# Attention scores through two three-bank PSUM tiles, with one exp per three key tiles into a ring

## Chip, core and metric

The kernel runs on one core of one Trainium2 chip. The metric is the device time of one execution in microseconds (us), median of several runs; lower is better. A profiled execution gives a trace with the start and length of each instruction on the engines: TensorE (PE, with its weight loads as PEld), VectorE (DVE), ScalarE (ACT), GpSimd (POOL) and SyncE (SP).

## The reference

Attention with normalised queries and keys, followed by a mixture of experts in which each token goes to one expert by a hash of its id. Batch 8, 12 heads, 448 tokens, head size 64; 3584 tokens of width 768, 8 experts of width 1024.

```python
q_n, k_n = (rmsnorm(q, g_q), rmsnorm(k, g_k))
scale = 1.0 / np.sqrt(q.shape[-1])
scores = scale * np.matmul(q_n, k_n.transpose(0, 1, 3, 2))
scores = scores - np.max(scores, axis=-1, keepdims=True)
attn = np.exp(scores)
attn = attn / (np.sum(attn, axis=-1, keepdims=True) + 1e-09)
return np.matmul(attn, v).astype(np.float32)
...
expert_idx = token_ids * np.int64(2654435761) % np.int64(E)
out = np.zeros((N, D), dtype=np.float32)
for e in range(E):
    mask = expert_idx == e
    if not mask.any():
        continue
    xe = x[mask]
    h = np.maximum(xe @ w1[e], 0.0)
    out[mask] = h @ w2[e]
```

## The kernel before

**Two stages.** First attention for all heads, with the routing tables computed beside it; then the experts, each with two matrix products over up to 512 gathered tokens. The attention result goes through a scratch tensor in HBM (`x_scratch`), is gathered per expert, turned by PE transposes, and the products are scattered to the output. The change lies in the attention stage.

**Steps and groups.** A step is one pair of heads of one batch element: 48 steps, `s` = 0 to 47. Steps come in groups, mostly of three, that share the preparation: squares of q and k on DVE (`prep_sq`), their sums by 16 matmuls against an identity on PE (`prep_sum`, line 287), a reduction on DVE (`prep_red`), an Ln and two exps on ScalarE (`prep_rr`), four products on DVE (`prep_norm`), and a copy of v (`prep_v`). For a group starting at step 3n the loop places one set of sums in the first and one in the second step of the group before or the one before that; a steady group of three steps therefore has two sets of sums, one Ln, and none in its third step.

**Scores.** The 448 keys of two heads make 3.5 tiles of 128 each. The kernel keeps them as seven key tiles per step (`SL = 7`): `score(s, j)` for j = 0, 1, 2 computes two tiles, one for each head, by two matmuls on 64 rows each, on the lower and on the upper half of the array (line 496); j = 3 computes the two half tiles as one matmul on all 128 rows (line 501). The scores go to a PSUM tile `sc_ps` of two banks, of which there are three. One exp takes both tiles of j = 0, 1, 2 (896 elements per partition, line 498), another the single tile of j = 3 (448, line 503). They write `expT`, one of two SBUF tiles of seven key tiles.

**AV.** `av_part(s, 0)` and `av_part(s, 1)` are 12 matmuls each (line 520), for one head each, `av_part(s, 2)` 8 more on half the columns (line 527), into the one PSUM tile `av_ps`; then DVE takes the reciprocal of the row sums and the product into `x_sb` (lines 535, 536). AV of a step runs one step after its scores.

**Transposes.** `transposes(s)` is eight PE transposes into the one PSUM bank `qkT_ps`, which it shares with the sums, and two DVE copies out of it, to kT and qT (lines 485, 487).

**Order.** It is written by hand (`manual_schedule`); each engine takes its instructions in that order in this loop. In step s (lines 688 to 709): scores j = 1 and 2, transposes of s + 1, score j = 3, AV parts 0 and 1 of s - 1, the `pre` and `mid` lists (v, squares, norms, sums), AV part 2 of s - 1, score j = 0 of s + 1, the `post` list (Ln and exps of `prep_rr`). So the six matmuls of j = 0, 1, 2 stand together on PE. After that, from step 14 on, one entry of `side` per step: eleven parts p1 to p11 of the routing, fourteen pairs of table columns (`table`, one DVE and one POOL operation for each column), and `table_mm` (28 matmuls). p3, p6 and `table_mm` each use a `sc_ps` tile. POOL issues the loads of q, k, v and weights and the gathers.

**PSUM.** Eight banks: six for `sc_ps`, one for `qkT_ps`, one for `av_ps`.

Of the kernel before, what the change touches and what calls it, by code (L numbers as in the profile page):

```python
# [8 lines left out]
FP32 = mybir.dt.float32  # L9
BF16 = mybir.dt.bfloat16  # L10
FP16 = mybir.dt.float16
I32 = mybir.dt.int32
AF = mybir.ActivationFunctionType
ALU = mybir.AluOpType
AX = mybir.AxisListType
PSUM = bass.MemoryType.PSUM
# [3 lines left out]
def kernel(  # L20
# [12 lines left out]
    nc = tc.nc  # L33

    B, H, S, D = q.shape
    N, DIN = out.shape
    E = moe_w1.shape[0]
    F = moe_w1.shape[2]
    P = 128
    HP = H // 2  # L40
    CO = DIN // P
    FO = F // P
    NTC = N // P
    HW = DIN // 2
    scale = 1.0 / float(D) ** 0.5
# [6 lines left out]
    NHI = E * KT + NOV  # L52
# [12 lines left out]
    SL = 7  # L65
# [129 lines left out]
            steps.append((gi, i))  # L195
    NG = len(groups)
    GMAX = 3

    with tc.manual_schedule(), \
         tc.tile_pool(name="a_nat", bufs=1) as a_nat, \  # L200
# [2 lines left out]
         tc.tile_pool(name="a_n8", bufs=2) as a_n8, \  # L203
         tc.tile_pool(name="a_v8", bufs=1) as a_v8, \
         tc.tile_pool(name="a_qk", bufs=3) as a_qk, \
         tc.tile_pool(name="a_exp", bufs=2) as a_exp, \
         tc.tile_pool(name="a_x", bufs=2) as a_x, \
         tc.tile_pool(name="rt_sb", bufs=1) as rt_sb, \
         tc.tile_pool(name="ps_qk", bufs=1, space=PSUM) as ps_qk, \
         tc.tile_pool(name="ps_sc", bufs=3, space=PSUM) as ps_sc, \  # L210
         tc.tile_pool(name="ps_av", bufs=1, space=PSUM) as ps_av:


# [3 lines left out]
        v_bufs = [a_nat.tile([P, 2 * HP, 8, D], BF16, name=f"vr_{t}") for t in range(NB)]  # L217
        v8_tiles = [a_v8.tile([P, GMAX, 8, DP], BF16, name=f"v8_{t}") for t in range(NV8)]

        first = a_exp.tile([P, SL, S], BF16, name="expT")[:].rearrange("p a s -> p (a s)")[  # L220
            :, 0:4 * 8 * D].bitcast(FP32).rearrange("p (a n s d) -> p a n s d", a=2, n=1, d=D)

        def runs(t, h0, hstep, nh, tok0, stride, cnt):
# [53 lines left out]
        def prep_sum(gi, a, wide=False):  # L277
            n = groups[gi][2]
            sq = st[gi].pop(("sq", a))
            m = 8 * n  # L280
            if wide:
                T = ps_sc.tile([P, 2, 512], FP32, name="sc_ps")[:, 0]
            else:
                T = ps_qk.tile([P, 512], FP32, name="qkT_ps")
            sp = T[:, 0:m * W].rearrange("p (s w) -> p s w", w=W)
            for c in range(NW):
                nc.tensor.matmul(sp, lhsT=ident16[:], rhs=sq[:, c, 0:m],  # L287
                                 start=(c == 0), stop=(c == NW - 1))
            st[gi]["sp", a] = sp
# [61 lines left out]
        slot_i = rt([P, NTC], I32, "slot_i")  # L351
        parts = rt([P, 2, NTC], I32, "parts")
        hl = rt([P, 2, NTC], FP32, "hl")
        lo1 = rt([P, NTC, P], FP16, "lo1")
        hi1 = rt([P, NTC, NHI], FP16, "hi1")
        V, G = nc.vector, nc.gpsimd
        rts = {}

# [13 lines left out]
            G.tensor_copy(oc[:], ot[:])  # L372

        def p3():
            ps = ps_sc.tile([P, 2, 512], FP32, name="sc_ps")[:, 0]
            oh = onehot[:].rearrange("p e c -> p (e c)")
            for h in range(2):
                nc.tensor.matmul(ps[0:KM, 2 * h:2 * h + 2], lhsT=oh[:, KM * h:KM * h + KM],
                                 rhs=sel2[:], start=True, stop=True)
            nc.tensor.matmul(ps[:, 8:8 + E], lhsT=emask[:], rhs=oc[:], start=True, stop=True)  # L380
            nc.tensor.matmul(ps[:, 8 + E:8 + 2 * E], lhsT=ones128[:], rhs=oc[:], start=True, stop=True)
            c4 = ps[0:KM, 0:4].rearrange("p (h k) -> p h k", k=2)
            V.tensor_copy(cmix[0:KM, :, 0:PL], c4[:, :, 0:1].to_broadcast([KM, 2, PL]))
            V.tensor_copy(cmix[0:KM, :, PL:P], c4[:, :, 1:2].to_broadcast([KM, 2, P - PL]))
            V.tensor_copy(et[:].rearrange("p a e -> p (a e)"), ps[:, 8:8 + 2 * E])  # L385
# [20 lines left out]
            G.tensor_tensor(out=add_e[:], in0=add_e[:], in1=base_e[:], op=ALU.subtract)  # L406

        def p6():
            ps = ps_sc.tile([P, 2, 512], FP32, name="sc_ps")[:, 0]
            oh = onehot[:].rearrange("p e c -> p (e c)")  # L410
            nc.tensor.matmul(ps[:, 0:E * NTC], lhsT=u128[:], rhs=oh, start=True, stop=False)
            for h in range(2):
                nc.tensor.matmul(ps[:, KM * h:KM * h + KM], lhsT=cmix[0:KM, h],
                                 rhs=tri[0:KM].rearrange("p e c -> p (e c)"),
                                 start=False, stop=(h == 1))
            V.tensor_tensor(out=rank[:], in0=ps[:, 0:E * NTC].rearrange("p (e c) -> p e c", e=E),
                            in1=bc(offl[:]), op=ALU.add)
# [27 lines left out]
                            scalar2=tv[:, c:c + 1], op0=ALU.is_equal, op1=ALU.mult)  # L445

        def table_mm():
            val = ps_sc.tile([P, 2, 512], FP32, name="sc_ps")[:, 0, 0:NHI]
            for c in range(NTC):
                nc.tensor.matmul(val, lhsT=lo1[:, c], rhs=hi1[:, c],  # L450
                                 start=(c == 0), stop=(c == NTC - 1))
            emp = rt([P, NHI], FP32, "emp")
            pos = rt([P, NHI], FP32, "pos")
            V.tensor_scalar(out=emp[:], in0=val, scalar1=0.0, scalar2=float(BIG),
                            op0=ALU.is_equal, op1=ALU.mult)
            V.tensor_scalar(out=pos[:], in0=val, scalar1=0.0, scalar2=-1.0,
                            op0=ALU.is_gt, op1=ALU.mult)
            V.tensor_tensor(out=emp[:], in0=emp[:], in1=pos[:], op=ALU.add)
            V.scalar_tensor_tensor(out=gidx[:], in0=val, scalar=float(N // 2), in1=emp[:],
                                   op0=ALU.add, op1=ALU.add)  # L460
# [20 lines left out]
        def transposed(s):  # L481
# [5 lines left out]
            nc.vector.tensor_copy(qT[:], T[:, 0:S])  # L487
            qkt[s] = (qT, kT)

        def score(s, j):  # L490
            qT, kT = qkt[s]
            expT = pend[s][0]
            sc = ps_sc.tile([P, 2, 512], FP32, name="sc_ps")
            if j < 3:
                for hh in range(2):
                    nc.tensor.matmul(sc[:, hh, :S], lhsT=kT[64 * hh:64 * hh + 64, P * j:P * j + P],  # L496
                                     rhs=qT[64 * hh:64 * hh + 64, :], start=True, stop=True)
                nc.scalar.activation(expT[:, 2 * j:2 * j + 2, :], sc[:, :, :S], AF.Exp,  # L498
                                     bias=0.0, scale=1.0)
            else:  # L500
                nc.tensor.matmul(sc[:, 0, :S], lhsT=kT[:, 384:512], rhs=qT[:, :],  # L501
                                 start=True, stop=True)
                nc.scalar.activation(expT[:, 6, :], sc[:, 0, :S], AF.Exp, bias=0.0, scale=1.0)  # L503
                qkt.pop(s)

        def av_part(s, part):
# [4 lines left out]
            if part == 0:  # L511
                av = ps_av.tile([P, SL, D + 1], FP32, name="av_ps")
                pend[s].append(av)
            expT, av = pend[s]
            tl = lambda hh, j: 6 if j == 3 else 2 * j + hh
            if part < 2:
                hh = part
                for t in range(3):
# [113 lines left out]
        side += [(lambda c=c: (table(c), table(c + 1))) for c in range(0, NTC, 2)]  # L632
        side += [table_mm]
        NS = len(steps)
        pend[0] = [a_exp.tile([P, SL, S], BF16, name="expT")]
        prep_sum(1, 0, True)
        prep_red(1, 0)
        score(0, 0)
# [10 lines left out]
        prep_v(0)  # L649
        transposed(1)  # L650
        zero_kv(nc.vector, v_bufs[0], HP, 2 * HP)
        pend[1] = [a_exp.tile([P, SL, S], BF16, name="expT")]
        score(1, 0)


# [27 lines left out]
        for s in range(1, NS):  # L683
            gi, i = steps[s]
            b, hp0, n = groups[gi]
            hp = hp0 + i
            nxt = s + 1 < NS
            score(s, 1)
            score(s, 2)
            if nxt:  # L690
                transposes(s + 1)
            score(s, 3)
            if s == NS - 1:
                for kt in range(KT - 1):
                    bank = ps_qk.tile([P, 512], FP32, name="qkT_ps")
                    put_xT(xg_e[kt], xT_e, kt, bank[:].bitcast(FP16)[:, 0:DIN])
            av_part(s - 1, 0)
            av_part(s - 1, 1)
            for f, *arg in pre[s]:
                f(*arg)  # L700
            for g, a in mid[s]:
                prep_sum(g, a)
                prep_red(g, a)
            av_part(s - 1, 2)
            if nxt:
                pend[s + 1] = [a_exp.tile([P, SL, S], BF16, name="expT")]
                score(s + 1, 0)
            for f, *arg in post[s]:
                f(*arg)
            if hp == 1 and b % 2 and b + 3 < B:  # L710
                load_qk(b + 3, 0, 2 * HP)
                load_v(b + 3, 0, 2 * HP)
            if side and s >= 14:
                side.pop(0)()
            if s == 24:
                n_ov = nc.values_load(novi[0:1, 0:1], min_val=0, max_val=NOV)
            if s == NS - 4:
                for kt in range(KT - 1):
                    gather(xg_e[kt], gidx[:, kt:kt + 1], N_EARLY)
            if hp == 3:  # L720
                if b == 3:
                    w_tiles[0] = [load_w1(0, w_pool)]
                if b == 4:
                    w_tiles[0].append(load_w2(0, w_pool))
                if b == 5:
                    w_tiles[1] = [load_w1(1, w_pool)]
                if b == 6:
                    w_tiles[1].append(load_w2(1, w_pool))
# [183 lines left out]
```

## Time and profile before

| | us |
|---|---|
| median of three runs (383.76 to 384.19) | 384.19 |
| the profiled execution | 386.59 |
| its span, first to last instruction | 385.0 |
| busy: PE, DVE, ACT, POOL | 344.5, 216.0, 187.5, 175.1 |
| attention steps with scores, first and last exp start | 12.8 to 185.53 |
| first to last Ln group read below, 12 groups of three steps | 49.04 to 171.21 |
| granted TensorE clock, 30 to 40 and 40 to 50 us | 0.74, 0.92 |

The profile page divides the span into 40 slices and prints tenths of busy time for each:

```profile
PE   7755998989999999999899999999998989999960
PEld 3443776766766777776667666666665656666630
DVE  5674789989999999988633233333222322232210
ACT  3753899989899999989321112212021111212200
```

A slice is 9.6 us. Up to about the nineteenth slice the core is in the attention stage, where PE, DVE and ScalarE are all near full; after it PE alone is. A matmul is recorded from its start to a modelled end, and matmuls overlap in the array, so distances between starts tell more about PE than busy time. The same holds in part for ScalarE and DVE, whose records overlap the next one's by some tenths of a microsecond.

### The profile page before, as it was taken

The page shows a single profiled execution, that of the slowest core. Times are in us where ns is not written, and L with a number is a line of the kernel's source. Part 1 is how long each engine was busy: PE and PEld are TensorE (multiplying, and loading weights), DVE is VectorE, ACT ScalarE, POOL GpSimd, SP SyncE. Part 2 cuts the span into 40 slices and gives each one's busy share as a digit, 9 for nine tenths or more (in the row PEclk, how much of TensorE's full clock was granted, in tenths as well). Part 3 has the DMA queues.
Part 4 walks back from the last instruction along what each step waited for, and adds up shares of the span by engine and source line. Part 5 has one row for each costly group of instructions (what it writes and reads, how often), then busy time and mean ns, then how long its engine had stood idle before and what let it go on. Part 6 is the DMA issues. An engine that isn't in the chain of part 4 may idle for free. (4 is left out here: it accounts for less than half of the span.)

```text
span 385.0 us, 9539 instructions
## 1 busy us (share of the span) xinstructions
PE 344.5 (89%) x4006; PEld 236.8 (62%) x4006; DVE 216.0 (56%) x519; ACT 187.5 (49%) x299; POOL 175.1 (45%) x247
## 2 busy tenths in 40 slices
PE   7755998989999999999899999999998989999960
PEld 3443776766766777776667666666665656666630
DVE  5674789989999999988633233333222322232210
ACT  3753899989899999989321112212021111212200
POOL 8998552014629950003347344462644636522030
PEclk9998899999999999999999999999999999999995
DMA  8999999943999999103548999999999999932030
GB/s 123 159 131 181 189 220 193 219 61 76 191 185 234 218 242 198 44 15 105 122 116 159 212 260 247 205 257 174 236 233 194 239 186 235 269 138 95 2 147 2
DMA packets 54269, 64.61 MB, mean 168 GB/s; under 512 B 22403, under 2 KB 42134, under 8 KB 53968
## 3 DMA queue, kind: packets, MB, share of 16 engines
q0 software_dynamic: 50592, 57.98, 85.8%
q1 hardware_dynamic: 3024, 5.41, 5.2%
q8 instruction: 32, 0.52, 0.6%
q10 hardware_dynamic: 608, 0.59, 0.5%
q14 instruction: 13, 0.11, 0.1%
HBM read 89.68 MB, written 18.09 MB: 280 GB/s over the span
## 5 line engine op out<-in xcount | busy, mean ns | idle before, releaser
L498 ACT ACTIVATE expT<-sc_ps 128x896 bf16<-128x896 f32 x144 | 123.9, 934 | 22.7 <-PE sc_ps L496 22.5
L765 PE MATMUL o_ps<-w_sb,h_sb 128*128 128x256 f16 (+1 forms) x512 | 87.9, 326 | 0.0
L752 PEld LDWEIGHTS <-w_sb 128*128 128x128 f16 x432 | 58.0, 144 | 25.7 <-issue 1.6
L752 PE MATMUL h_ps<-xT,w_sb 128*128 128x512 f16 x336 | 73.7, 379 | 0.0
L765 PEld LDWEIGHTS <-h_sb 128*128 128x128 f16 x512 | 48.9, 98 | 32.6
L173 POOL DMA_INDIRECT xg<-x_scratch,gidx x32 | 32.6, 1020 | 63.5 <-DVE x_sb L536 38.3
L770 POOL DMA_INDIRECT out_dram<-o_sb,gidx x32 | 33.0, 1031 | 51.5 <-ACT o_sb L769 17.0
L756 ACT ACTIVATE h_sb<-h_ps 128x512 f16<-128x512 f32 (+2 forms) x36 | 19.7, 550 | 75.1 <-PE h_ps L752 75.1
L758 DVE TENSOR_SCALAR h_sb<-h_ps 128x512 f16<-128x512 f32 (+2 forms) x36 | 22.8, 632 | 55.6 <-PE h_ps L752 55.6
L769 ACT COPY o_sb<-o_ps 128x768 f32<-128x768 f32 x16 | 12.8, 799 | 76.0 <-PE o_ps L765 51.3
L520 PEld LDWEIGHTS <-expT 128*128 128x128 bf16 x1152 | 42.5, 98 | 9.9 <-issue 6.0
L496 PE MATMUL sc_ps<-qT,kT 64*128 64x448 f16 x288 | 43.3, 358 | 4.5 <-DVE et L385 1.4
L520 PE MATMUL av_ps<-v,expT 128*128 128x65 bf16 x1152 | 44.0, 194 | 0.0
L769 DVE COPY o_sb<-o_ps 128x768 f32<-128x768 f32 x16 | 15.3, 958 | 45.7 <-PE o_ps L765 21.2
L816 POOL DMA_DIRECT2D w_sb<-in_moe_w_dram x36 | 23.1, 645 | 30.2 <-DMA w_sb<-in_moe_w_dram 28.2
L475 PE MATMUL qkT_ps<-ident,n 128*128 128x128 f16 x384 | 30.6, 222 | 5.4 <-DVE n L320 3.8
L475 PEld LDWEIGHTS <-n 128*128 128x128 f16 x384 | 22.3, 98 | 19.8 <-issue 11.9
L536 DVE TENSOR_TENSOR x_sb<-av_ps,srec 128x448 f16<-128x448 f32 x48 | 29.7, 619 | 1.5
L287 PEld LDWEIGHTS <-ident 128*128 128x128 f16 x544 | 24.6, 99 | 8.8 <-issue 6.8
L185 DVE COPY xT<-xT_ps 128x768 f16<-128x768 f16 x28 | 15.5, 554 | 23.9 <-PE xT_ps L184 23.8
L485 DVE TENSOR_SCALAR kT<-qkT_ps,g_col 128x512 f16<-128x512 f16 x48 | 23.1, 481 | 9.5 <-PE qkT_ps L475 8.4
L503 ACT ACTIVATE expT<-sc_ps 128x448 bf16<-128x448 f32 x48 | 27.7, 577 | 1.2 <-PE sc_ps L501 1.2
(140 smaller groups left out, 382.5 us busy)
## 6 DMA issues: line engine op xcount, KB each, us to landing
w_sb<-in_moe_w_dram POOLq DMA_DIRECT2D x32, 384.0 KB, 13.6
w_sb<-in_moe_w_dram POOLq DMA_DIRECT2D x12, 768.0 KB, 13.5
x_scratch<-x_sb SPq DMA_DIRECT2D x15, 288.0 KB, 6.1
w_sb<-in_moe_w_dram POOLq DMA_DIRECT2D x2, 1536.0 KB, 16.4
kr<-in_k_dram POOLq DMA_DIRECT2D x6, 384.0 KB, 9.0
qr<-in_q_dram POOLq DMA_DIRECT2D x3, 768.0 KB, 14.5
vr<-in_v_dram POOLq DMA_DIRECT2D x6, 384.0 KB, 19.4
kr<-in_k_dram POOLq DMA_DIRECT2D x6, 288.0 KB, 8.9
```

Source lines behind the costliest of these rows:

```text
L173: nc.gpsimd.indirect_dma_start(out=xg[:], out_offset=None, in_=x_dram[0:rows, :], in_offset=bass.IndirectOffsetOnAxis(ap=idx, axis=0), bou ...
L287: nc.tensor.matmul(sp, lhsT=ident16[:], rhs=sq[:, c, 0:m], start=(c == 0), stop=(c == NW - 1))
L475: nc.tensor.transpose(T[:, o:o + P], n8[:, a, i, j].rearrange("p h d -> p (h d)"), ident16[:])
L496: nc.tensor.matmul(sc[:, hh, :S], lhsT=kT[64 * hh:64 * hh + 64, P * j:P * j + P], rhs=qT[64 * hh:64 * hh + 64, :], start=True, stop=True)
L498: nc.scalar.activation(expT[:, 2 * j:2 * j + 2, :], sc[:, :, :S], AF.Exp, bias=0.0, scale=1.0)
L503: nc.scalar.activation(expT[:, 6, :], sc[:, 0, :S], AF.Exp, bias=0.0, scale=1.0)
L520: nc.tensor.matmul(av[:, 2 * t + hh, :], lhsT=expT[:, tl(hh, j), P * t:P * t + P], rhs=v8[:, i, 4 * hh + j, 0:D + 1], start=(j == 0), stop ...
L536: nc.vector.tensor_tensor(out=x_sb[:, :, hp * D:hp * D + D], in0=av[:, :, :D], in1=srec[:, :, None].to_broadcast([P, SL, D]), op=ALU.mult)
L752: nc.tensor.matmul(h_ps[:, :c1 - c0], lhsT=w1v[:, co, fo, :], rhs=xT[:, co, c0:c1], start=(co == 0), stop=(co == CO - 1))
L765: nc.tensor.matmul(o_ps[:, d0:d1], lhsT=h_sb[:, fo, col * P:(col + 1) * P], rhs=w2_sb[:, fo, d0:d1], start=(fo == 0), stop=(fo == FO - 1))
L769: (nc.vector.tensor_copy if col % 2 else nc.scalar.copy)(o_sb[:], o_ps[:])
L770: scat = nc.gpsimd.indirect_dma_start(out=out[:, :], out_offset=bass.IndirectOffsetOnAxis(ap=idx, axis=0), in_=o_sb[:], in_offset=None, bo ...
```

## The change

- The score tiles of all steps are numbered through, t = 7s + 2j + hh. Three successive ones share a PSUM tile of three banks (`GT = 3`), of which there are two. A tile that is begun in one step is finished in the next one where 7 is not a multiple of 3 (`filling` holds it).
- When the third is written, one exp takes all three (1344 elements per partition). Three steps then have seven exps instead of twelve, 112 in all instead of 192.
- The exps write one ring of 21 key tiles (`RING`), three steps' worth, in place of two tiles of seven. AV reads from the ring. The first group's raw q and k, which lay in an `expT` tile, lie in the ring.
- The order in a step: the transposes of s + 1 come between scores j = 1 and j = 2, score j = 3 between AV parts 0 and 1, and score j = 0 of s + 1 ahead of `pre`, `mid` and AV part 2. In the last step the three transposes of gathered tokens come ahead of score j = 3.
- The routing tables `lo1` and `hi1` lie in a weight tile of the pool that expert 0's and 1's second weights use.
- Users of a `sc_ps` tile other than scores (wide sums at the start, p3, p6, `table_mm`) take one of the two three-bank tiles.

```diff
@@ -195,6 +195,8 @@
     GMAX = 3
+    GT = 3
+    RING = GT * SL
@@ -203,11 +205,11 @@
-         tc.tile_pool(name="a_exp", bufs=2) as a_exp, \
+         tc.tile_pool(name="a_exp", bufs=1) as a_exp, \
...
-         tc.tile_pool(name="ps_sc", bufs=3, space=PSUM) as ps_sc, \
+         tc.tile_pool(name="ps_sc", bufs=2, space=PSUM) as ps_sc, \
@@ -217,7 +219,8 @@
-        first = a_exp.tile([P, SL, S], BF16, name="expT")[:].rearrange("p a s -> p (a s)")[
+        ring = a_exp.tile([P, RING, S], BF16, name="expT")
+        first = ring[:].rearrange("p a s -> p (a s)")[
@@ -279,7 +282,7 @@
-                T = ps_sc.tile([P, 2, 512], FP32, name="sc_ps")[:, 0]
+                T = ps_sc.tile([P, GT, 512], FP32, name="sc_ps")[:, 0]
@@ -351,8 +354,9 @@
-        lo1 = rt([P, NTC, P], FP16, "lo1")
-        hi1 = rt([P, NTC, NHI], FP16, "hi1")
+        tab = w_pool.tile([P, FO, DIN], FP16, name="w2_sb")[:].rearrange("p a b -> p (a b)")
+        lo1 = tab[:, 0:NTC * P].rearrange("p (c s) -> p c s", s=P)
+        hi1 = tab[:, NTC * P:NTC * (P + NHI)].rearrange("p (c s) -> p c s", s=NHI)
@@ -372,7 +376,7 @@
         def p3():
-            ps = ps_sc.tile([P, 2, 512], FP32, name="sc_ps")[:, 0]
+            ps = ps_sc.tile([P, GT, 512], FP32, name="sc_ps")[:, 0]
...
@@ -487,20 +491,22 @@
+        filling = []
+
         def score(s, j):
             qT, kT = qkt[s]
-            expT = pend[s][0]
-            sc = ps_sc.tile([P, 2, 512], FP32, name="sc_ps")
-            if j < 3:
-                for hh in range(2):
-                    nc.tensor.matmul(sc[:, hh, :S], lhsT=kT[64 * hh:64 * hh + 64, P * j:P * j + P],
-                                     rhs=qT[64 * hh:64 * hh + 64, :], start=True, stop=True)
-                nc.scalar.activation(expT[:, 2 * j:2 * j + 2, :], sc[:, :, :S], AF.Exp,
-                                     bias=0.0, scale=1.0)
-            else:
-                nc.tensor.matmul(sc[:, 0, :S], lhsT=kT[:, 384:512], rhs=qT[:, :],
-                                 start=True, stop=True)
-                nc.scalar.activation(expT[:, 6, :], sc[:, 0, :S], AF.Exp, bias=0.0, scale=1.0)
+            for hh in range(2 if j < 3 else 1):
+                t = SL * s + 2 * j + hh
+                if t % GT == 0:
+                    filling.append(ps_sc.tile([P, GT, 512], FP32, name="sc_ps"))
+                rows = slice(64 * hh, 64 * hh + 64) if j < 3 else slice(0, P)
+                nc.tensor.matmul(filling[0][:, t % GT, :S], lhsT=kT[rows, P * j:P * j + P],
+                                 rhs=qT[rows, :], start=True, stop=True)
+                if t % GT == GT - 1:
+                    r = (t + 1 - GT) % RING
+                    nc.scalar.activation(ring[:, r:r + GT, :], filling.pop()[:, :, :S], AF.Exp,
+                                         bias=0.0, scale=1.0)
+            if j == 3:
                 qkt.pop(s)
@@ -511,8 +517,9 @@
-            expT, av = pend[s]
-            tl = lambda hh, j: 6 if j == 3 else 2 * j + hh
+            av, = pend[s]
+            expT = ring
+            tl = lambda hh, j: (SL * s + (6 if j == 3 else 2 * j + hh)) % RING
@@ -686,25 +693,25 @@
             score(s, 1)
-            score(s, 2)
             if nxt:
                 transposes(s + 1)
-            score(s, 3)
+            score(s, 2)
             if s == NS - 1:
                 for kt in range(KT - 1):
                     bank = ps_qk.tile([P, 512], FP32, name="qkT_ps")
                     put_xT(xg_e[kt], xT_e, kt, bank[:].bitcast(FP16)[:, 0:DIN])
             av_part(s - 1, 0)
+            score(s, 3)
             av_part(s - 1, 1)
+            if nxt:
+                pend[s + 1] = []
+                score(s + 1, 0)
             for f, *arg in pre[s]:
                 f(*arg)
             for g, a in mid[s]:
                 prep_sum(g, a)
                 prep_red(g, a)
             av_part(s - 1, 2)
-            if nxt:
-                pend[s + 1] = [a_exp.tile([P, SL, S], BF16, name="expT")]
-                score(s + 1, 0)
             for f, *arg in post[s]:
                 f(*arg)
```

More of the change, by code (lines that the diff above doesn't have):

```diff
@@ L408, in p6 @@
         def p6():
-            ps = ps_sc.tile([P, 2, 512], FP32, name="sc_ps")[:, 0]
+            ps = ps_sc.tile([P, GT, 512], FP32, name="sc_ps")[:, 0]
             oh = onehot[:].rearrange("p e c -> p (e c)")
@@ L447, in table_mm @@
         def table_mm():
-            val = ps_sc.tile([P, 2, 512], FP32, name="sc_ps")[:, 0, 0:NHI]
+            val = ps_sc.tile([P, GT, 512], FP32, name="sc_ps")[:, 0, 0:NHI]
             for c in range(NTC):
@@ L634 @@
         NS = len(steps)
-        pend[0] = [a_exp.tile([P, SL, S], BF16, name="expT")]
+        pend[0] = []
         prep_sum(1, 0, True)
@@ L651 @@
         zero_kv(nc.vector, v_bufs[0], HP, 2 * HP)
-        pend[1] = [a_exp.tile([P, SL, S], BF16, name="expT")]
+        pend[1] = []
         score(1, 0)
```

## The prediction

> **What bounds the kernel now.** I read the windows first, cut at the exp that precedes each Ln on ScalarE (one Ln per head-pair group, three steps), to see which engine is full in the attention stage. The columns are start:end, length, then busy us and instruction count of PE, PEld, DVE, ACT and POOL, then granted clock, DMA share and GB/s.
>
> ```profile
> 69.17:78.97 9.80, 9.52 (x177) 6.92 (x173) 9.08 (x23) 9.28 (x16) 0.26 (x2) 1.00 1.54 219
> ...
> 141.04:150.83 9.79, 9.51 (x177) 6.92 (x173) 9.69 (x28) 9.27 (x15) 0.00 (x0) 1.00 1.09 222
> ...
> sum 122.17, PE 115.40 PEld 84.64 DVE 114.80 ACT 112.41 POOL 46.63; mean PE 9.62 PEld 7.05 DVE 9.57 ACT 9.37 POOL 3.89
> ```
>
> The second window shows DVE at its fullest. The sum line covers the twelve groups from 49.04 to 171.21 us. Three engines are nearly full, so a busy share decides nothing, and I went to the groups and then to the order in time.
>
> ```profile
> L498 ACT ACTIVATE expT<-sc_ps 128x896 bf16<-128x896 f32 x144 | 123.9, 934 | 22.7 <-PE sc_ps L496 22.5
> ```
>
> The 144 wide exps wait 22.5 us in all for score matmuls, over half of it before 43 us, while loads set the pace. In a steady group the wait is 0.49 us, once:
>
> ```profile
> 69.17 0.92 ACT L498 ACTIVATE expT<-sc_ps 128x896 bf16<-128x896 f32 x1 [0.45 <-PE sc_ps L496]
> ...
> 70.62 1.71 ACT L498 ACTIVATE expT<-sc_ps 128x896 bf16<-128x896 f32 x2
> 72.22 0.55 ACT L503 ACTIVATE expT<-sc_ps 128x448 bf16<-128x448 f32 x1
> 72.64 2.54 ACT L498 ACTIVATE expT<-sc_ps 128x896 bf16<-128x896 f32 x3
> 75.04 0.58 ACT L503 ACTIVATE expT<-sc_ps 128x448 bf16<-128x448 f32 x1
> ...
> 78.97 0.92 ACT L498 ACTIVATE expT<-sc_ps 128x896 bf16<-128x896 f32 x1 [0.49 <-PE sc_ps L496]
> ```
>
> ```profile
> 74.90 1.14 PE L496 MATMUL sc_ps<-qT,kT 64*128 64x448 f16 x6
> 75.97 0.62 PE L475 MATMUL qkT_ps<-ident,n 128*128 128x128 f16 x8
> 76.48 0.35 PE L501 MATMUL sc_ps<-qT,kT 128*128 128x448 f16 x1
> 76.67 0.91 PE L520 MATMUL av_ps<-v,expT 128*128 128x65 bf16 x24
> 77.47 0.85 PE L287 MATMUL qkT_ps<-sq_q,ident 128*128 128x96 f16 x16
> 78.25 0.32 PE L527 MATMUL av_ps<-v,expT 128*64 128x65 bf16 x8
> 78.50 0.74 PE L496 MATMUL sc_ps<-qT,kT 64*128 64x448 f16 x6
> ```
>
> Read together these show the ring that sets 9.80 us a group: ScalarE runs without a gap from 69.17 to the j=3 exp at 75.04; only its end frees the PSUM tile for the third pair of the burst at 74.90 (75.68 in the trace); PE then needs 2.82 us (transposes, j=3 score, 24 AV, 16 sums, 8 AV) to the next burst at 78.50, and the exp starts 0.47 later. 6.51 + 2.82 + 0.47 = 9.80. It is a ring through ScalarE, a PSUM tile and PE's order, not one engine. In steps without sums the period is 2.82 us (j=0 exps at 177.50, 180.32, 183.13), ScalarE alone.
>
> **What the Trainium skill says.** "ScalarE: Activation LUTs", section "What ACT_TABLE_LOAD costs": an ACTIVATE with immediates takes 186 ns + 0.833 ns per element, and neighbours overlap by about 93 ns. The trace agrees on the length (934 against 932) but shows more overlap: starts 0.797 us apart at 896 elements, 0.425 at 448, so a launch costs hardly anything beyond its elements. "TensorEngine Tiling (Array Packing)", section "Tiling Modes", Key Properties: changing the tiling mode drains TensorE. The trace agrees. The routing table's matmuls stand between two score pairs there:
>
> ```profile
> 160.16 0.36 PE L496 MATMUL sc_ps<-qT,kT 64*128 64x448 f16 x2
> 160.46 0.99 PE L450 MATMUL sc_ps<-hi,lo 128*128 128x64 f16 x28
> 161.38 0.36 PE L496 MATMUL sc_ps<-qT,kT 64*128 64x448 f16 x2
> ```
>
> Pair to full-array matmul takes 0.30 us where pair to pair takes 0.19, and the last of the 28 to the next pair takes 0.126 where their own spacing is 0.029: 0.10 us for each change of mode. "Perfetto Trace Analysis", section "Optimizing Scalar/DVE Operations": where ScalarE isn't saturated but causes bubbles elsewhere, smaller instructions let work finish sooner. The change goes the other way.
>
> **The change part by part.** *Fewer exps.* Three steps had nine exps of 896 and three of 448: 9 x 0.797 + 3 x 0.425 = 8.45 us; now seven of 1344, each 0.797 + 0.372 = 1.17: 8.19. With the 0.64 of Ln and rr the ScalarE floor goes from 9.09 to 8.83. At most 0.26 a group, if ScalarE were the bound.
>
> *PE's order.* The three score pairs of a step stood in one burst (0.68 us to the transposes); now s1 (first pair of the step), transposes, s2, half the AV, s3, other half, next step's s0, sums, last AV. Each lone pair changes mode on both sides. In starts: pair to what follows 0.29, transposes 0.45 + 0.10, AV half 12 x 0.031 = 0.37 (+ 0.10 ahead of a pair), s3 0.19, last AV 0.25, sums 0.78. A step is 0.29 + 0.55 + 0.29 + 0.37 + 0.19 + 0.47 + 0.29 + 0.25 = 2.70, a group with its two sums 9.66. Before: 0.68 + 0.51 + 0.19 + 0.80 + 0.78 + 0.25 = 3.21 twice and 2.47 without sums, 8.89. So PE's own work rises by 0.77 a group. The full-to-pair change after transposes and AV is not in the trace of before; its bounds are 0 and 0.10, and I take 0.10 from the routing table.
>
> *Two PSUM tiles in place of three.* The first matmul of a fill waits for the exp two fills back. From the last matmul of a fill to that release: 0.47 to the exp's start (78.50 to 78.97), 1.29 for the exp (0.92 + 0.37), 0.05 to PE (exp of 0.91 from 173.46, pair at 174.42): 1.81 us. Number a cycle's 21 tiles; fills are 0-2, 3-5, ... 18-20. PE's own way from a fill's last matmul to the first of the fill after next is: tile 20 to tile 3: s3 0.19, AV 0.47, s0 0.29, AV 0.25 = 1.20, short by 0.61; tile 11 to tile 15: 0.29 + 0.37 + 0.19 + 0.47 = 1.32, short by 0.49; tile 2 to 6 1.50, but the 0.61 lies inside; the others 2.16 or more, enough. Both waits lie on PE with everything queued behind them (transposes, AV, sums), and so DVE's evacuations. 9.66 + 0.61 + 0.49 = **10.76 us a group**. ScalarE, at 8.83, then waits about 1.9. DVE fits: its starts show 1.475 a step (kT 0.40, qT 0.30, reciprocal 0.235, product 0.54) plus norms 1.87, squares 1.74, v 0.47, reductions 0.33 = 8.83, and 9.79 with a table part in each step.
>
> *PSUM tiles for routing.* Parts 3 and 6 (after steps 16 and 19) take one of the two tiles while the other is half filled, so fill 18-20 must follow the exp of 15-17 in the same tile: 1.81 - 0.84 = 0.97 each, plus their matmuls, 0.25 and 0.42. The table's 28 matmuls cost 1.0 with nothing half filled. Together 3.6; before, groups with these are inside the 122.17.
>
> *Edits at nothing.* The exps' ring: a slot is rewritten three steps later, its readers are done one step later. The first raw q/k lie in the ring, read before step 0's scores exist. Routing tables in a weight tile: expert 1's w2 load on POOL waits for the table's matmuls, which the step issues just ahead of it; behind it on POOL stand only gathers of later steps, it lands in 16.4 us, and it is used some 40 us later. Without that cover it would be the lateness itself.
>
> *Sum.* Twelve groups: 12 x 10.76 + 3.6 = 132.7 against 122.17: +10.5. Last five steps without sums: PE 8.10 a cycle with waits 0.61, 0.43, 0.43 = 9.57 against 3 x 2.82: +1.1 for three, taken as +1.5 for the tail. In the last step the three xT transposes (184.44 to 187.06) come ahead of the last score, whose exp then delays the last AV by 0 to 1.0: +0.5. Up to 49 us loads set the pace (exps idle 6.55 us until 37.91), but after it one group runs partly at half clock: +0.5. The expert stage is shifted, not changed. **+13.0 us**: span 385.0 to 398.0, that execution 386.6 to 399.6. The median of the runs is 2.4 below the profiled one, and I carry the difference over: 384.19 + 13 = about 397.
>
> **Rivals.** *Mode changes hidden.* If lone pairs cost 0.19 with their weights loaded ahead, PE has 8.46, the waits grow to 0.81 and 0.69, a group is 9.96: 119.5 + 3.6 = 123.1 for the twelve, and with +2.5 for the rest about 388. Against it: weights of a score pair load only 4 ns before it at 140.57. *The exp isn't late.* If the buffer came back within 1.20 us of the last matmul, both waits vanish and a group is 9.66: 119.5 against 122.2, tail -0.5: about 381, faster. It decides from a return of 1.20 down; the parts above say 1.81, and the exp alone is 1.29. For it speaks that the 0.49 us wait of ScalarE does go. *DVE couples in.* Transposes now follow the sums within 0.8 us and share one PSUM bank with them, so they wait for DVE's reduction behind a norm; at 0.7 us more a group, some 405. *Not what it says.* If the whole ring counted as one buffer, every AV would wait for the newest exp, over 1 us a step: above 430. [...]I give it little.
>
> **How the numbers follow.** Forecast case 0.65, mode changes hidden 0.14, exp not late or a gain in another way 0.12, DVE coupling or the ring as one buffer 0.07, no change that can be seen 0.02. About 0.2% is what a measurement of this kernel can tell from none. So faster 0.12, same 0.03, slower 0.85. The unknown mode changes (half of 0.6 a group: -4), the tail (1), DVE (+6) give 391 to 404 for the forecast case alone; with the hidden case in, 387 to 405.
>
> **What would show it.** Exp mean near 1.3 us, 112 of them; groups between Lns near 10.8 us; PE idle for expT ahead of tiles 3 and 15 of each 21, near 0.6 and 0.5 us; score pairs 0.29 from what follows; ScalarE idle near 1.9 us a group. It is wrong if Lns stand 9.8 us apart or less, or if PE's waits name DVE.

## The result, with the profile after

| | before | after |
|---|---|---|
| median of four runs each | 383.98 | 394.96 |
| lowest, highest | 382.53, 384.19 | 393.12, 397.75 |
| ratio, 95% interval | | 1.03 [1.0227, 1.0373] |
| the profiled execution | 386.59 | 393.12 |
| its span | 385.0 | 391.5 |

The changed kernel is 3% slower, 11.0 us between the medians; the forecast was 397 from 384.19. The profiled executions lie only 6.5 us apart in span, and a split by stage says why. Marks are the starts of the group Lns, the first expert matmul behind the last AV (a few of the first expert's run ahead of it) and the end; all in us.

| stretch | before | after | difference | forecast |
|---|---|---|---|---|
| start to the fifth group Ln | 49.86 | 48.54 | -1.3 | +0.5 |
| twelve groups from there | 122.17 | 131.40 | +9.2 | +10.5 |
| last group Ln to the first expert matmul | 18.39 | 20.21 | +1.8 | +2.0 |
| expert stage | 194.6 | 191.4 | -3.2 | 0 |

The expert stage belongs to the one execution, not to the change: in that profile of before PE waited there 2.3 us in all for gathers, which after's didn't. Of the ten other profiles taken below, all with the same expert code, seven have 190.4 to 192.2 us for it, and the other three, 192.5 to 195.0, have 1.9 to 2.5 us of the same wait. The attention groups are the change.

First the windows of two groups of after, from Ln to Ln: one without routing work, one with table columns on DVE. Columns as in the windows of before.

```profile
70.44:81.09 10.65, 10.44 (x175) 6.92 (x173) 9.46 (x23) 9.55 (x12) 0.25 (x2) 1.00 1.42 193
157.73:168.37 10.64, 10.43 (x182) 7.09 (x181) 10.07 (x28) 9.53 (x11) 0.00 (x0) 1.00 0.26 68
```

Both kinds take the same 10.65 us, where the same two groups of before take 9.79 each. (Over the ten groups compared below the means are 10.95 after and 10.20 before, as those with other routing work are longer in both.) ScalarE has fewer exps and fills a smaller part of the group. The page's rows of the exp and of the score matmuls, in the format of before:

```profile
L507 ACT ACTIVATE expT<-sc_ps 128x1344 bf16<-128x1344 f32 x112 | 142.7, 1289 | 26.6 <-PE sc_ps L503 24.2
...
L503 PE MATMUL sc_ps<-qT,kT 64*128 64x448 f16 (+1 forms) x336 | 79.4, 363 | 6.9 <-ACT expT L507 4.8
```

112 exps of 1289 ns, and PE now names the exp as what its score matmuls wait for. Where that happens is in PE's order in time (start, length, instructions, in brackets the idle time before and who ended it):

```profile
130.79 0.35 PE L503 MATMUL sc_ps<-qT,kT 128*128 128x448 f16 x1
...
131.74 0.32 PE L534 MATMUL av_ps<-v,expT 128*64 128x65 bf16 x8
131.98 0.36 PE L503 MATMUL sc_ps<-qT,kT 64*128 64x448 f16 x1
132.52 0.35 PE L503 MATMUL sc_ps<-qT,kT 64*128 64x448 f16 x1 [0.17 <-ACT expT L507]
132.79 0.62 PE L479 MATMUL qkT_ps<-ident,n 128*128 128x128 f16 x8
...
136.86 0.36 PE L503 MATMUL sc_ps<-qT,kT 64*128 64x448 f16 x2
...
138.22 0.72 PE L503 MATMUL sc_ps<-qT,kT 64*128 64x448 f16 x2
138.87 0.85 PE L290 MATMUL qkT_ps<-sq_k,ident 128*128 128x96 f16 x16
```

And ScalarE's in the same group:

```profile
131.17 3.87 ACT L507 ACTIVATE expT<-sc_ps 128x1344 bf16<-128x1344 f32 x3 [0.22 <-PE sc_ps L503]
...
137.25 2.64 ACT L507 ACTIVATE expT<-sc_ps 128x1344 bf16<-128x1344 f32 x2 [0.25 <-PE sc_ps L503]
```

The matmul at 130.79 writes tile 20 and completes a fill. Its exp starts at 131.17, lasts 1.29, and PE's first matmul into that buffer, tile 3, starts at 132.52: a return of 1.73 us. PE had arrived at 131.98; the two matmuls of that pair, which otherwise start within 0.01 us of each other, stand 0.54 apart. The second place is hidden in a merged line: the pair at 138.22 takes 0.72 instead of 0.36 because its second matmul, tile 15, starts at 138.59. The exp that frees its buffer follows the pair at 136.86 and starts at 137.25: 1.73 again, PE 0.37 early. So a group loses 0.54 + 0.37 = 0.91 us on PE, twice in 21 tiles.

The list of waits, restricted to the ten groups from 70.44 to 179.94, shows how little of that a reader would find there:

```profile
PE sc_ps L503 <- ACT expT L507: 1.7, 10, 0.2
```

It counts 1.7 us, all at the first place. By the distances of starts 8.3 us are lost: 0.53 or 0.54 at tile 3 in each of the ten groups, and at tile 15 0.37 to 0.40 in seven of them, 0.01 to 0.15 in the other three. At both places, in all ten, the matmul starts 0.05 or 0.06 us after the end of its exp. The modelled 0.36 us of the pair's first matmul covers most of each wait, and the wait at 138.22 has no idle bracket at all.

### The profile page after: what moved, and what is told of

The parts are those of the page before. It is cut to its first block, busy times and chain, and to the rows that moved or that the text cites. A ratio compares the mean times of both kernels' runs of the same rounds, so it can differ in the third digit from the quotient of the medians.

```text
span 391.5 us, 9436 instructions
## 1 busy us (share of the span) xinstructions
PE 358.7 (92%) x4006; PEld 237.6 (61%) x4006; DVE 220.3 (56%) x519; ACT 190.0 (49%) x219; POOL 175.0 (45%) x247
## 5 line engine op out<-in xcount | busy, mean ns | idle before, releaser
L507 ACT ACTIVATE expT<-sc_ps 128x1344 bf16<-128x1344 f32 x112 | 142.7, 1289 | 26.6 <-PE sc_ps L503 24.2
L503 PE MATMUL sc_ps<-qT,kT 64*128 64x448 f16 (+1 forms) x336 | 79.4, 363 | 6.9 <-ACT expT L507 4.8
L527 PEld LDWEIGHTS <-expT 128*128 128x128 bf16 x1152 | 44.1, 99 | 15.9 <-issue 5.5
L527 PE MATMUL av_ps<-v,expT 128*128 128x65 bf16 x1152 | 52.9, 196 | 0.3 <-DVE x_sb L543 0.3
L290 PEld LDWEIGHTS <-ident 128*128 128x128 f16 x544 | 23.6, 98 | 13.6 <-issue 13.1
L503 PEld LDWEIGHTS <-kT 64*128 64x128 f16 (+1 forms) x336 | 19.0, 94 | 13.0 <-issue 2.4
```

The costliest lines, as they stand in the source:

```text
L290: nc.tensor.matmul(sp, lhsT=ident16[:], rhs=sq[:, c, 0:m], start=(c == 0), stop=(c == NW - 1))
L503: nc.tensor.matmul(filling[0][:, t % GT, :S], lhsT=kT[rows, P * j:P * j + P], rhs=qT[rows, :], start=True, stop=True)
L507: nc.scalar.activation(ring[:, r:r + GT, :], filling.pop()[:, :, :S], AF.Exp, bias=0.0, scale=1.0)
L527: nc.tensor.matmul(av[:, 2 * t + hh, :], lhsT=expT[:, tl(hh, j), P * t:P * t + P], rhs=v8[:, i, 4 * hh + j, 0:D + 1], start=(j == 0), stop ...
```

## The experiments

The runs came in three batches. The kernel before took 391.61, 390.49 and 383.62 us in the three, so every ratio is against the kernel before of the same batch; the last section says what of that difference the profiles show. Beside the ratio I give the time of the same ten groups, seventh group Ln to the seventeenth, through which the TensorE clock is 1.00 in the profiles, but for two stretches of 3.4 us in the one of the old order and for much of the one with the exp split inside its tile: 102.04 us before, 109.50 after. The kernel before was profiled once, so all are held against that one reading. "Plain", or "quiet", is the first of them, without routing work; "table" one of the late ones, with table columns on DVE: 9.79 and 9.79 before, 10.65 and 10.64 after.

**The changed kernel again**, in the second batch.

> The changed kernel unaltered, on the same chip as the other runs of this call. Theory: 2.5 to 3.5% over before, quiet groups 10.65 us.

400.07 us, ratio 1.0248 [1.0173, 1.0323]; ten groups 109.41, plain 10.65, table 10.65. The loss in these ten groups came back, 7.4 us.

**The order alone.** Before, with the changed order of a step; three tiles of two banks and the old exps stay. A third `expT` tile and the tables in a weight tile make room.

```diff
             score(s, 1)
-            score(s, 2)
             if nxt:
                 transposes(s + 1)
-            score(s, 3)
+            score(s, 2)
...
             av_part(s - 1, 0)
+            score(s, 3)
             av_part(s - 1, 1)
+            if nxt:
+                pend[s + 1] = [a_exp.tile([P, SL, S], BF16, name="expT")]
+                score(s + 1, 0)
```

> The kernel before with the changed order of a step alone: lone score pairs between transposes, AV halves and sums, but three two-bank PSUM tiles, the old exps of 896 and 448, expT tiles (three, since the earlier score j = 0 meets an expT tile still being read). Theory (the two-tile return on top of the mode changes): PE has 9.66 us a group, the return with three tiles (1.44 us) is never late, so groups stand 9.7 us apart where nothing else is in the way and the time is 381 to 385, no slower than before. Rival (the order with its lone pairs is what costs): groups near 10.6 and 392 to 396.

391.71 us, ratio 1.0021 [0.9993, 1.0049]; ten groups 102.28. The windows of a plain and a table group:

```profile
71.02:80.77 9.75, 9.75 (x175) 6.92 (x173) 9.13 (x23) 9.54 (x15) 0.25 (x2) 1.00 1.53 217
152.55:162.56 10.01, 9.80 (x178) 7.06 (x177) 9.86 (x28) 9.60 (x15) 0.00 (x0) 1.00 0.28 72
```

In the plain group PE is busy for 9.75 of 9.75 us, and no matmul in it waits. That is PE's own length of the new order, forecast at 9.66 and 0.77 above the old one; it costs nothing there, since the ring of before was 9.79 long anyway. In the table group DVE is at 9.86 of 10.01 and 0.2 us are lost. The lone score pairs are therefore paid for, but from slack.

**The two PSUM tiles with the old order.** After, with only the loop of a step put back.

```diff
             score(s, 1)
+            score(s, 2)
             if nxt:
                 transposes(s + 1)
-            score(s, 2)
+            score(s, 3)
...
             av_part(s - 1, 2)
+            if nxt:
+                pend[s + 1] = []
+                score(s + 1, 0)
```

> The changed kernel with the old order of a step: the score pairs j = 0, 1, 2 in one burst, exps of three tiles into the ring, two PSUM tiles. Theory: PE has 8.87 us a group, but now tile 6 of 21 comes 0.82, tile 12 1.43 and tile 18 1.43 us ahead of its PSUM tile, so a group takes about 12.5 us and the time is 412 to 422. Rival (the order is what costs): 384 to 390, near before.

421.45 us, ratio 1.076 [1.0681, 1.0839]; ten groups 127.17, quiet ones 12.2. PE's order in time:

```profile
163.97 0.74 PE L503 MATMUL sc_ps<-qT,kT 64*128 64x448 f16 x5
165.72 0.35 PE L503 MATMUL sc_ps<-qT,kT 64*128 64x448 f16 x1 [1.01 <-ACT expT L507]
...
168.53 0.55 PE L503 MATMUL sc_ps<-qT,kT 64*128 64x448 f16 x4
170.27 0.36 PE L503 MATMUL sc_ps<-qT,kT 64*128 64x448 f16 x2 [1.19 <-ACT expT L507]
```

With six score matmuls in one burst little lies between a fill and the fill after next. In a quiet group PE stands idle twice for over 1 us, as in these lines, and once more for 0.38. So the new order doesn't cost the 3%; without it the tiles would cost 7.6%.

**Three tiles of two banks, with ring and new order.** After, with exps of two key tiles.

```diff
-    GT = 3
-    RING = GT * SL
+    GT = 2
+    RING = 22
...
-         tc.tile_pool(name="ps_sc", bufs=2, space=PSUM) as ps_sc, \
+         tc.tile_pool(name="ps_sc", bufs=3, space=PSUM) as ps_sc, \
```

> The changed kernel with its order and ring, but fills of two key tiles in three two-bank PSUM tiles (168 exps of 896, ring of 22). Theory: the waits for a PSUM tile go (return 1.44 us against 2.0 or more on PE's own way), a group is PE's 9.66: 381 to 386. Rival (order, or the ring in one buffer, costs): 390 to 396.

391.86 us, ratio 1.0012 [0.9983, 1.004]; ten groups 102.53, plain 9.95, table 9.81 and 10.21. Everything of the change is in it but the size of a PSUM tile and of its exp, and the loss is gone. Its groups look uneven only from Ln to Ln: from score matmul to score matmul on PE the plain one takes 9.75 and two table ones 10.01, the same as with the order alone. The ring isn't the cause either.

**Only the early score.** Before, with j = 0 of the next step ahead of `pre`, `mid` and AV part 2, the burst of six thus broken once.

```diff
             av_part(s - 1, 1)
+            if nxt:
+                pend[s + 1] = [a_exp.tile([P, SL, S], BF16, name="expT")]
+                score(s + 1, 0)
...
             av_part(s - 1, 2)
-            if nxt:
-                pend[s + 1] = [a_exp.tile([P, SL, S], BF16, name="expT")]
-                score(s + 1, 0)
```

> The kernel before with one edit of the order: score j = 0 of the next step ahead of the sums and the last AV part, scores j = 1 and 2 still together; three PSUM tiles, old exps, three expT tiles. Theory: one lone pair more (0.2 us a step) makes PE 9.27 us a group, ScalarE has 9.09 and no longer waits for the sums, so quiet groups go from 9.80 to about 9.35 and those with a table part stay at DVE's 9.8: 378 to 382, faster than both kernels. Rival (DVE or the mode changes take it back): 384 or more, groups at 9.8.

389.76 us, ratio 0.9949 [0.9912, 0.9986]; ten groups 101.13. The same kernel in the third batch, with more runs:

> The kernel before with one move alone: the first score of the next step ahead of what precedes the halves of AV (three exp tiles, routing tables in a weight tile), run again in more rounds. My theory: ScalarE's wait of about 0.5 us a step group goes, quiet groups about 9.46 instead of 9.80, 0.3 to 0.8% under the kernel before. Rival (the first reading was scatter): within 0.2% of it.

384.02 us, ratio 1.0007 [0.9984, 1.0031]; ten groups 100.67. The windows of this second profile:

```profile
69.96:79.45 9.49, 9.33 (x175) 6.80 (x173) 9.13 (x23) 9.31 (x16) 0.25 (x2) 1.00 1.54 213
150.33:160.18 9.85, 9.52 (x178) 6.78 (x175) 9.75 (x28) 9.45 (x17) 0.00 (x0) 1.00 0.29 73
```

The plain group does get shorter, 9.49 against 9.79, but the table groups don't: DVE is at 9.75 of 9.85 us. In the ten groups 0.9 and 1.4 us remain, and the whole kernel's gain didn't come back in the second reading. I don't call this version faster than the kernel before.

**Routing parts out of the score tiles.** After, with p3, p6 and `table_mm` in the bank of the transposes.

```diff
         def p3():
-            ps = ps_sc.tile([P, GT, 512], FP32, name="sc_ps")[:, 0]
+            ps = ps_qk.tile([P, 512], FP32, name="qkT_ps")
...
```

> The changed kernel with routing parts 3 and 6 and the table's matmuls in the one-bank PSUM tile of the transposes instead of one of the two score tiles. Theory: the two groups with parts 3 and 6, 11.62 and 11.13 us, lose most of the 0.97 us that each part made fill 18-20 wait, to 10.7 to 11.0; other groups unchanged. Rival (their cost is DVE's and POOL's work of those parts): 11.1 to 11.6 as before.

402.24 us in a single run; groups with p3, p6 and the table 12.18, 11.66 and 12.60 where after has 11.62, 11.13 and 11.57. Worse, not better. PE around p3:

```profile
84.03 0.26 PE L382 MATMUL qkT_ps<-sel,onehot 128*112 128x2 bf16 x2 [0.51 <-DVE ss L298]
...
85.28 0.62 PE L479 MATMUL qkT_ps<-ident,n 128*128 128x128 f16 x8 [0.64 <-DVE et L389]
```

The part waits for DVE's reduction out of that bank, and the next transposes for DVE's reading of the part. So this bank is no better place. What the parts cost in a score tile this run can't say, as it brings waits of its own; the trace of after can. There the part p3 waits 0.19 us for an exp, and the fill behind it waits not for an exp but for DVE's reading of the part:

```profile
86.54 0.36 PE L503 MATMUL sc_ps<-qT,kT 64*128 64x448 f16 x2 [0.40 <-DVE et L389]
```

**The exp of three split inside its PSUM tile.** After, with an exp of 896 behind the second key tile and one of 448 behind the third, both from the one three-bank tile.

```diff
-                if t % GT == GT - 1:
-                    r = (t + 1 - GT) % RING
-                    nc.scalar.activation(ring[:, r:r + GT, :], filling.pop()[:, :, :S], AF.Exp,
+                if t % GT == 1:
+                    r = (t - 1) % RING
+                    nc.scalar.activation(ring[:, r:r + 2, :], filling[0][:, 0:2, :S], AF.Exp,
+                                         bias=0.0, scale=1.0)
+                if t % GT == 2:
+                    nc.scalar.activation(ring[:, t % RING, :], filling.pop()[:, 2, :S], AF.Exp,
```

> The changed kernel with each exp of three key tiles cut in two: one of 896 as soon as two of the three are written, one of 448 after the third. Order, ring and the two three-bank PSUM tiles stay. Theory (the PSUM tile comes back too late): from a fill's last matmul to the return it is 0.47 + 0.57 + 0.05 = 1.09 us instead of 1.81, less than PE's own 1.20 and 1.32, so both waits go though there are 112 exps more (ScalarE 9.19 us a group): quiet groups 9.65 to 9.75 instead of 10.64, the time level with before within 0.7%. Rival (two tiles or the lone pairs cost as such, not the length of the exp): groups stay near 10.6, 2 to 3% over before.

535.55 us (four runs of 501.76 to 537.94), a miss by far. The profile is of the run of 537.94, with groups of about 20.5 us and a mean TensorE clock of 0.80. The clock is the smaller part: two groups that lie wholly at 1.00 take 16.92 us each from score matmul to score matmul, against 10.65 in after. PE first, then ScalarE:

```profile
115.49 0.36 PE L503 MATMUL sc_ps<-qT,kT 64*128 64x448 f16 x1
116.85 0.35 PE L503 MATMUL sc_ps<-qT,kT 64*128 64x448 f16 x1 [1.00 <-ACT expT L507]
```

```profile
115.88 0.92 ACT L507 ACTIVATE expT<-sc_ps 128x896 bf16<-128x896 f32 x1 [0.80 <-PE sc_ps L503]
117.23 0.54 ACT L510 ACTIVATE expT<-sc_ps 128x448 bf16<-128x448 f32 x1 [0.43 <-PE sc_ps L503]
```

The third key tile's matmul, in a bank of its own, starts 0.05 us after the end of the exp of the first two, as it does in 111 of the 112 fills: the order between matmul and exp is kept for the whole PSUM tile, not for its banks. The edit thus added a wait of its own, in each fill, and says nothing on the question. So the next one uses separate tiles.

**The same split in separate tiles.** After, with two tiles of two banks and two of one bank; six banks as before.

```diff
                 if t % GT == 0:
-                    filling.append(ps_sc.tile([P, GT, 512], FP32, name="sc_ps"))
+                    filling.append(ps_sc.tile([P, 2, 512], FP32, name="sc_ps"))
+                if t % GT == 2:
+                    filling.append(ps_s1.tile([P, 1, 512], FP32, name="s1_ps"))
...
-                if t % GT == GT - 1:
-                    r = (t + 1 - GT) % RING
-                    nc.scalar.activation(ring[:, r:r + GT, :], filling.pop()[:, :, :S], AF.Exp,
+                if t % GT > 0:
+                    w = 2 if t % GT == 1 else 1
+                    r = (t + 1 - w) % RING
+                    nc.scalar.activation(ring[:, r:r + w, :], filling.pop()[:, :, :S], AF.Exp,
```

> The kernel after, with each three-bank tile cut into two PSUM tiles in the same six banks: a two-bank tile (two of them) with one exp of 896 after the second key tile, and a one-bank tile (two of them) with one exp of 448 after the third. Order of PE, ring, routing tables as in the kernel after; 112 exps more. My theory (the loss is the return of a PSUM tile, long because one exp of 1344 frees three banks at once): the two-bank tile is back 0.47 + 0.92 + 0.05 = 1.44 us after its last matmul, before PE's own way has come to the tile that takes it, the single one likewise after about 1.0; both waits of 0.54 and 0.36 us in a group vanish, quiet groups 9.6 to 9.8 us instead of 10.64, and the time is within 0.7% of the kernel before, although ScalarE does more instructions. Rival 1 (the lone pairs and changed modes of PE, or the ring, cost it): groups stay at 10.5 to 10.7, 2 to 3% slower than before. Rival 2 (ScalarE is the bound): groups longer than 10.64, since it has 112 instructions more.

385.57 us, ratio 1.007 [1.0038, 1.0103]; ten groups 103.01. Windows of a plain and a table group:

```profile
71.36:81.11 9.75, 9.75 (x176) 6.92 (x174) 9.13 (x23) 9.40 (x18) 0.25 (x2) 1.00 1.36 202
153.40:163.40 10.00, 9.79 (x184) 7.19 (x182) 9.85 (x28) 9.59 (x18) 0.00 (x0) 1.00 0.28 72
```

PE's order in the two groups, where the single tile is called `s_ps`:

```profile
77.05 0.32 PE L538 MATMUL av_ps<-v,expT 128*64 128x65 bf16 x8
77.30 0.36 PE L506 MATMUL s_ps<-qT,kT 64*128 64x448 f16 x1
77.30 0.36 PE L506 MATMUL sc_ps<-qT,kT 64*128 64x448 f16 x1
77.59 0.62 PE L480 MATMUL qkT_ps<-ident,n 128*128 128x128 f16 x8
...
157.17 0.61 PE L480 MATMUL qkT_ps<-ident,n 128*128 128x128 f16 x8 [0.21 <-DVE ss L299]
```

The pair that stood 0.54 apart starts together, and so, within 0.01 us, does that of tiles 14 and 15. Order, ring, routing tables and banks are those of after, ScalarE has 112 instructions more, and the plain group falls from 10.65 to 9.75, PE's own length. In the table groups it is 10.00, above the 9.6 to 9.8 that I had expected: there the transposes wait 0.21 us for DVE's reduction, with DVE at 9.85. The ratio lies at the edge of what I had allowed. How many tiles there are and how long their exps last changed together, here and with three tiles of two banks: three tiles of three banks don't fit into the eight, so the two weren't told apart.

**A burst broken once, on three tiles with ring.** After with two-tile fills (as above), and the order of only the early score.

```diff
             score(s, 1)
+            score(s, 2)
             if nxt:
                 transposes(s + 1)
-            score(s, 2)
+            score(s, 3)
...
             av_part(s - 1, 0)
-            score(s, 3)
             av_part(s - 1, 1)
```

> Two-tile fills in three PSUM tiles, ring of 22, with scores j = 1 and 2 together and j = 0 of the next step ahead of the sums (the order of the run with score j = 0 early). Theory: PE's 9.27 us a group bounds it, ScalarE has 9.01; quiet groups near 9.4, those with table parts at DVE's 9.8; 0.3 to 0.8% under before. Rival (rarer exps free ScalarE, which was the bound): 1% or more under before.

394.65 us, ratio 1.0092 [1.0067, 1.0117]; ten groups 104.35. I had hoped for a kernel better than before and missed it. One reason is in PE's order:

```profile
157.75 0.55 PE L503 MATMUL sc_ps<-qT,kT 64*128 64x448 f16 x3
158.56 0.35 PE L503 MATMUL sc_ps<-qT,kT 64*128 64x448 f16 x1 [0.26 <-ACT expT L507]
```

As seven key tiles of a step don't divide by two, in every other step a fill ends in the middle of a pair. At one such place in six steps the second matmul of the pair waits for a buffer that the first didn't need: starts 0.6 us apart, five times in the ten groups. That is up to 3 of the 3.2 and 3.7 us that these groups take beyond the two readings of only the early score. Whether it counts in full wasn't settled.

## Why the prediction was right, and where it was off

The sign, the mechanism and both places of the wait are as forecast; what is off are sizes.

- **PSUM tiles' return, the term that decides.** Forecast 1.81 us, measured 1.73 at both places. The exp's 1.29 and the 0.05 to PE hold; what differs is the start of the exp after the last score matmul, 0.38 and 0.39 in place of the 0.47 read from a burst of before. The waits are 0.54 and 0.37, not 0.61 and 0.49.
- **PE's own order.** Forecast 9.66 us a group, measured 9.75 with the waits gone (order alone, and split in separate tiles). It includes the full-to-pair change of 0.10, for which before had only the routing table to show: in after the transposes at 132.79 reach the next pair at 133.35, 0.56 against the 0.55 of the sum. The rival of hidden mode changes is out.
- **A group.** 9.75 + 0.54 + 0.37 = 10.66 against 10.65 measured and 10.76 forecast. Two errors of opposite sign: PE's order 0.09 short, the waits 0.19 too long. ScalarE's idle time, a sign that was named too, reads 1.1 us in the window (9.55 busy of 10.65) and not 1.9, as an exp is recorded for 1.29 us where the next can start after 1.17; by starts it is 10.65 - 8.83 = 1.8.
- **Which part of it costs.** In the ten groups the order alone is +0.2 us, order with ring and three tiles +0.5, all of it with the fills in separate tiles +1.0, the whole change +7.5. So the size of tile and exp makes six and a half to seven of the 7.5. The "Perfetto Trace Analysis" page of the Trainium skill, section "Optimizing Scalar/DVE Operations", says that breaking up instructions of an engine that isn't saturated but causes bubbles may let work finish sooner; the split in separate tiles is that case, 10.65 to 9.75 us. Split inside one tile it did the opposite.
- **Routing parts.** Forecast 0.97 + 0.25, 0.97 + 0.42 and 1.0; measured over a quiet group 0.97, 0.48 and 0.92. The step that failed is "fill 18-20 must follow the exp of 15-17 in the same tile". In after that fill takes the tile that the part has just left, and waits for DVE's reading of the part: the matmul at 86.54 starts before the exp of 15-17, from 85.63 for 1.29, is over. All excess over twelve quiet groups, 131.40 - 12 x 10.65 = 3.6, equals the forecast only by chance: two groups of 11.28 and 11.15, somewhat long in before too (10.04 and 10.34), fill it up. Against before p3's group loses least of the ten, 0.25 us, since before takes 11.37 for it.
- **Start and tail.** -1.3 against +0.5, which the runs don't explain. This stretch differs from one execution to the next: the two profiles of only the early score reach the fifth group Ln after 49.29 and 45.67 us. The tail is 1.8 against 2.0.
- **The exp isn't late.** The separate tiles come nearest to this rival's condition, as both waits go. It would not have given 381: plain groups go to 9.75 and table groups to 10.00, where DVE binds. So DVE's coupling is real, 0.25 us a group there, but in after it doesn't show: plain and table groups both take 10.65.
- **Ring and tables at nothing.** The ring held, as three tiles with it are level with before. Nor does it count as one buffer: in the ten groups of after AV waits for no exp. The wait of POOL for the table's matmuls, 27.9 us ahead of one weight load, delayed nothing that PE named.

## What to carry to other kernels

With a double-buffered PSUM tile, add up its return (last matmul to the evacuation's start, the evacuation, release) and lay it beside what the producing engine has to do between that matmul and the first one into the same buffer. A larger evacuation saves launches; here, where that other work was shorter at two of the seven fills of a cycle, it lost more than it saved. So the comparison has to be made for each position in the cycle. The evacuating engine can have a sixth of its time free (1.8 of 10.65 us here) and still set the period. Where an order is packed to the last tenth, look for waits in the distances of starts, since busy times that are modelled ends cover them.

## What the runs showed of the hardware

- A launch of an exp is almost free beside its elements. The closest starts in the trace are 1.17 us apart for 1344 elements, as forecast, where before has 0.797 for 896 and 0.424 for 448, together 1.22. The three lie 0.373 apart for 448 elements more each, so a launch is worth some 0.05 us. Seven exps in place of twelve save 0.26 us in a group of ten, so there was little to win from the start.
- A PSUM tile that is partly read while another of its banks is to be written: 0.05 us from the exp's end to the matmul, in 111 of 112 fills, as if they were one buffer. Whether the chip or the program's order between tiles asks for it wasn't tried.
- The TensorE clock can fall to half outside of the load-paced start. In the batch where before took 391.61 us, the profile of the order alone has, at the border to the expert stage:

```profile
186.70:196.90 10.20, 7.63 (x81) 5.28 (x78) 4.96 (x12) 4.44 (x6) 1.92 (x3) 0.50 0.42 92
```

A clock of 0.50 for 10.2 us; six of the eight profiles of that batch and the next have such a stretch there, of 10.2 to 13.7 us, and those of the third, on the same chip as the first, have none. With it the stretch from the last group Ln to the first expert matmul takes 25.4 to 28.2 us, without it 18.4 to 20.2 in before, after and the third batch. That is about the distance between the batches, though before itself has no profile in them. The clock isn't the first event there: in each of the six PE, DVE and ScalarE stand idle together for 0.36 to 1.13 us, beginning 1.6 to 5.1 us before it falls; in the four others they nowhere do so for 0.3 us. What stops them isn't shown. This border is why no whole time is compared across batches.
